# A planned attention and convolution kernel: other durations and weights in the planner, and one score unit for the last 64 keys of two chunks

## The chip, the cores and the metric

The kernel runs on one core of one Trainium2 chip. The metric is the device time of one execution in microseconds (us). An execution has five instruction streams: TensorE (PE in the profile, with its weight loads PEld), VectorE (DVE), ScalarE (ACT), GpSimd (POOL) and SyncE (SP).

## The reference

Two stages, in eight batches of 3136 rows:

```python
scores = (1/S) * z @ z.T                  # z: 3136 x 64
attn   = maximum(scores, 0) ** 2
x      = u * (attn @ v)                   # u, v: 3136 x 256
x1, x2, x3 = split(x @ w_proj, 3)         # 256 columns each
conv   = irfft(rfft(x2) * rfft(filter))   # along the 3136 rows
out    = (x1 * conv * x3) @ w_out
```

There is no softmax: a score is taken through ReLU and squared, and the score matrix is symmetric.

## The kernel before

**Tiles.** The 3136 rows are 25 tiles of 128 keys. The last tile (`NT - 1`, number 24) holds only 64 keys; its other 64 partitions carry the same keys again. The rows are also cut into seven chunks of queries, `CHUNKS = (512, 512, 512, 512, 512, 256, 320)`. A batch goes through its chunks in order.

**Score units.** For each chunk `entries(c)` (L1448) lists the key tiles in units, mostly two tiles to a unit. `score_mm` (L1484) multiplies 64 rows of z by the chunk's columns, one tile into each of the two PSUM banks of a pair. The 64 contraction rows fill half of the array: the first tile of a unit uses the upper half, the second the lower half. ScalarE applies ReLU to both banks in one instruction (L1672, PSUM into the tile `R`), and ScalarE or VectorE squares it (L1679 or L1681, `R` into `A`, bf16). Part of the score blocks come from the symmetry instead, by DMA transposes (`mirror`, L1583).

**Weighing.** `weigh` (L1500) multiplies `A` with v into two PSUM accumulators `ps_o`, one for each half of v's columns. The 64 keys of tile 24 are weighed apart by `weigh_short` (L1627), two half-array matmuls for a chunk, appended to the score group that comes `DELAY = 4` groups after the unit with tile 24 (`ends_at`, L1620). VectorE takes the accumulators out, in two halves, with the factor u (L1722, into `xT`).

**The last tile in chunks 0 to 3.** In these chunks tile 24 is a unit of its own, `(24,)`, in the middle of the chunk's list: one matmul, one bank used of the pair that it takes, a ReLU and a square over 512 columns.

**The second stage.** `add_proj` (L1023) projects `xT` (ReLU-free copies by either engine at L498 and L502, the gate product by VectorE in two halves at L1059), `add_spectrum` (L1113) and `add_end` (L1224) do the convolution by two-step transforms and the output projection. This is work of the kinds FA, FB and FZ, in the same streams as the scores (S) and the weighing (W).

**The planner.** The order of every stream is made when the program is built. Each piece of work is a `Task` with a cost on each engine that could run it, what it depends on, and the buffers that it takes. `Plan.go` (L309) runs the tasks through a model in time and emits them in the order that results. Its costs are linear: `c_act(n)`, `c_dve(n)`, `c_pe(n)` (L44 to L57). Going from S to other PE work or back adds a constant (L325). What the diff touches:

- `pick_pe` (L247) chooses PE's next task. While in S it stays there as long as the next score task can start within `STAY`; from other work it enters S when two pairs of banks are free, three where the W work on hand is over `AMPLE`; while it waits for pairs it takes W, and F work too where W on hand is over `BACKLOG`. F goes ahead of W while a credit is positive, which each W task raises by `PACE`, and while the queued work of ScalarE and VectorE (`queued`, L243) is under `FULL`.
- `pick` (L287) gives work that two engines could do to the second of them if it ends there earlier than on the first; `YIELD` adds the wait that this would cause to work that only that engine can do.
- `both` (L507) gives such work its two costs. The squares name VectorE first (L1688), nearly all PSUM copies ScalarE first.

Of the kernel before, what the change touches and what calls it, by code (L numbers as in the profile page):

```python
# [21 lines left out]
KR = 2 * N2  # L22
KC = 100
CHUNKS = (512, 512, 512, 512, 512, 256, 320)
PACE = 0.6
HOLD = 3
DELAY = 4
GROUP = 1
BACKLOG, AMPLE, STAY = 2.0, 4.0, 0.1
LATE_PUT, LATE_LOAD, LATE_TURN, LATE_C, LATE_D2 = 3.0, 1.0, 1.5, 2.5, 1.0  # L30
SPEC_LAG = 1
LATE_F = 6.0
# [1 line left out]
FINAL = (0, 2, 4, 6, 1, 3, 5)  # L34
ZP, ZL = 0, 0.0
MOST = 3
FULL = 3.0
YIELD = 1.0
REACH = 2
INF = float("inf")  # L40
ISSUED = "issued"


def c_act(n):  # L44
    return 0.055 + n * 0.000833


def c_dve(n):
    return 0.068 + n * 0.00104
# [110 lines left out]
class Plan:  # L160
# [148 lines left out]
    def go(self):  # L309
        while True:  # L310
            got = []
            x = self.pick_pe()
            if x:
                got.append((x[0], 0, x[1], "PE", x[2]))
            for i, e in enumerate(self.pend):
                x = self.pick(e)
                if x:
                    got.append((x[0], i + 1, x[1], e, None))
            if not got:
                break  # L320
            start, _, task, e, k = min(got, key=lambda g: g[:2])
            if k:
                self.queues[k].remove(task)
                if (k == "S") != (self.mode == "S") and self.mode:
                    start += 0.11  # L325
                self.mode = k
                if k == "W":
                    self.credit = min(self.credit + PACE, 2.0)
                elif k != "S":
                    self.credit = max(self.credit - task.cost["PE"], -2.0)  # L330
            self.run(task, e, start)
        left = sum(len(q) for q in self.queues.values()) + sum(len(q) for q in self.pend.values())
        assert not left, f"{left} tasks left over"
# [3 lines left out]
def kernel(  # L337
# [56 lines left out]
    v_p = Pool("v16", 2, [P, VW], BF16)  # L394
    R_p = Pool("R", 2, [P, 2, 512], F32)
    A_p = Pool("A", 8, [P, 1024], BF16)
    M_p = [Pool("M1", 1, [P, 2048], BF16), Pool("M2e", 1, [P, 2048], BF16), Pool("M2o", 1, [P, 2048], BF16)]
    xT_p = Pool("xT", 8, [P, 2, 512], BF16)
    g_p = Pool("gate", 26, [P, 512], BF16)
    x1_p = Pool("x1", 2, [P, 512], BF16)  # L400
    x2_p = Pool("x2", 2, [P, 2 * D], BF16)
    s1_p = Pool("s1", 3, [P, 2, D], BF16)
# [89 lines left out]
    def on(engine, emit, cost, deps=(), takes=(), **kw):  # L492
        return job(None, lambda e: emit(), {engine: cost}, deps, takes, **kw)
# [529 lines left out]
    def add_proj(b, c, xt, xt_tasks):  # L1023
# [7 lines left out]
        def to_gates():  # L1031
            for nb in range(2):
                box = {}

                def mm1(nb=nb, box=box):
                    box["p"] = bank()
                    box["x"] = x1_p.tile()
                    for k in range(2):
                        matmul(
                            box["p"][:, :cw], wp16[:, k, ds(nb * P, P)], xt["t"][:, k, :cw],  # L1040
                            start=(k == 0), stop=(k == 1),
                        )

                def ev1(e, box=box):
                    box["made"] = copy(e, box["x"][:, :cw], box["p"][:, :cw])

                def mm3(nb=nb, box=box):
                    box["p3"] = bank()
                    gates[b, c, nb] = g_p.tile()
                    for k in range(2):  # L1050
                        matmul(
                            box["p3"][:, :cw], wp16[:, k, ds((4 + nb) * P, P)], xt["t"][:, k, :cw],
                            start=(k == 0), stop=(k == 1),
                        )

                def ev3(nb=nb, box=box):
                    for h, w in halves(c):
                        g, p, x = (by_half(y, h, w) for y in (gates[b, c, nb], box["p3"], box["x"]))
                        got = nc.vector.tensor_tensor(g[:, ::-1] if h == 0 else g, p, x, ALU.mult)  # L1059
                        made.setdefault((b, c, nb), []).append(has_read(got, p, [box["made"]]))  # L1060

                a = pe(kind, mm1, c_pe(cw, cw), xt_tasks, [one_slots, x1_p.slots])
                if late and c in AFTER:
                    put_back.append(a)
                e1 = job(None, ev1, both(cw), [a], prio=late)
                e1.frees.append((a, 0))
                a3 = pe(kind, mm3, c_pe(cw, cw), [*xt_tasks, a], [one_slots, g_p.slots])
                e3 = on("DVE", ev3, c_dve(cw), [a3, e1], prio=late)
                e3.frees += [(a3, 0), (a, 1)]
                users.extend([a, a3])  # L1070
                gtasks.append((a3, e3))
# [375 lines left out]

    def entries(c):  # L1448
        skip = [t for a in mirrored(c) for t in tiles[a]]
        todo = [t for t in range(NT) if t not in skip]  # L1450
        pairs = []
        for a in range(c + 1, min(c + REACH, NC - 1) + 1):
            pairs += [tuple(tiles[a][i : i + 2]) for i in range(0, len(tiles[a]) - 1, 2)]
        rest = [t for t in todo if all(t not in x for x in pairs)]
        wide = 4 if 4 * CHUNKS[c] <= 1024 else 2
        rest = [tuple(rest[i : i + wide]) for i in range(0, len(rest), wide)]
        sends = [x for x in rest if any(c < home[t] <= c + REACH for t in x)]
        pairs = sorted(pairs + sends, key=lambda x: min(home[t] for t in x if home[t] > c))
        rest = [("S", x) for x in rest if x not in sends]
        pairs = [("S", x) for x in pairs]  # L1460
        taken = [("M", tuple(tiles[a][i : i + 2])) for a in mirrored(c) for i in range(0, len(tiles[a]), 2)]
        mid = [x for x in rest + pairs if NT - 1 in x[1]]
        rest, pairs = ([x for x in got if x not in mid] for got in (rest, pairs))
        h = len(rest) // 2
        if not pairs:
            got = spread(rest, taken)
            i = got.index(rest[h])
            return got[:i] + mid + got[i:]
        return spread(rest[:h], taken) + mid + spread(rest[h:], pairs)
# [6 lines left out]
    groups = [scored[i : i + GROUP] for i in range(0, len(scored), GROUP)]  # L1476
    mirrors, mirror_tasks = {}, {}

    def blocks(x, n, cw):
        if n <= 2:  # L1480
            return x[:, 0:n, :cw]
        return x[:].rearrange("p i j -> p (i j)")[:, 0 : n * cw].rearrange("p (i j) -> p i j", i=n)

    def score_mm(un, where):  # L1484
        b, c, k = un
        cw = CHUNKS[c]
        ps = ps_t[where]
        zt = zT[b]
        pair = plans[b, c][k][1]
        order = (0, 1) if len(pair) <= 2 else (0, 2, 1, 3)  # L1490
        for i in order[: len(pair)] if len(pair) != 3 else (0, 2, 1):
            t, h, m = pair[i], ds((i if len(pair) <= 2 else i // 2) * dqk, dqk), P
            matmul(
                blocks(ps, len(pair), cw)[:m, i], zt[h, ds(t * P, m)], zt[h, ds(C0[c], cw)], start=True, stop=True
            )
        live[un] = ps

    acc, full = {}, {}
# [121 lines left out]
    ends_at, scored_by = {}, {}  # L1620
    for gi, g in enumerate(groups):
        for b, c, k in g:
            if NT - 1 in plans[b, c][k][1]:
                ends_at.setdefault(min(gi + DELAY, len(groups) - 1), []).append((b, c))
    short, chunk_w, tails = {}, {}, {}

# [10 lines left out]
    for gi, g in enumerate(groups):  # L1637
# [15 lines left out]
            for x in more:  # L1653
                weigh_short(*x)

        costs = [c_pe(CHUNKS[un[1]]) for un in g]
        extra = sum(c_pe(CHUNKS[c]) for _, c in more)
        st = pe("S", sg, sum(costs) + extra, deps, [pair_slots] * len(g))
        tails[gi] = st
# [1 line left out]
        for i, un in enumerate(g):  # L1661
            b, c, k = un
            cw = CHUNKS[c]
            pair = plans[b, c][k][1]
            rows, n = P, len(pair)
            last = k == len(plans[b, c]) - 1
            box = {}

# [2 lines left out]
                p = blocks(live[un], n, cw)[:rows]  # L1671
                has_read(nc.scalar.activation(blocks(box["R"], n, cw)[:rows], p, AF.Relu), p)  # L1672

            def sq(e, un=un, rows=rows, n=n, cw=cw, box=box):
                A = A_p.tile()
                r = blocks(box["R"], n, cw)[:rows]
                a = A[:rows, 0 : n * cw].rearrange("p (i j) -> p i j", i=n)
                if e == "ACT":
# [6 lines left out]
                "ACT", relu, c_act(n * cw), [(st, -sum(costs[i + 1 :]) - extra)], [R_p.slots], prio=0  # L1685
            )
            r_.frees.append((st, i))
            how = {"DVE": c_dve(n * cw)} if (b, c) == (0, 0) and k > 1 else both(n * cw, "DVE")  # L1688
            q_ = job(None, sq, how, [r_], [A_p.slots], prio=1)
            q_.frees.append((r_, 0))  # L1690
            if c == NC - 1 and last or gi == len(groups) - 1:
                if b == 0:
# [1 line left out]
                else:  # L1694
                    st.frees.append((z_tasks[b][0], 0))
            mirror(un, q_)
            if NT - 1 in pair:
                short[b, c] = q_, un, pair.index(NT - 1)
            if all(x == "M" for x, _ in plans[b, c][:k]):
                for j in range(k):  # L1700
                    add_mirrored((b, c, j))
# [5 lines left out]
            if last:  # L1707
# [3 lines left out]
                for dh in range(2):  # L1711

                    def xe(dh=dh, b=b, c=c, cw=cw, xt=xt):
# [8 lines left out]
                            nc.vector.scalar_tensor_tensor(x, f, inv_s2, ut, ALU.mult, ALU.mult)  # L1722

                    x_ = on(
                        "DVE", xe, c_dve(cw), [w_last[dh], u_tasks[b, c], *((d, ISSUED) for d in evs)], [xT_p.slots] if dh == 0 else [], prio=-1
                    )
                    evs.append(x_)
                    x_.frees.append(w_first[dh])
# [45 lines left out]
    for gi, got in ends_at.items():  # L1774
        for b, c in got:
# [3 lines left out]
                join(tails[gi], t, ISSUED)  # L1779
            for t in chunk_w[b, c][1]:  # L1780
                join(t, tails[gi], ISSUED)
            if plans[b, c][un[2]][1] != (NT - 1,):
                q_.holders += 1
            tails[gi].frees.append((q_, 0))
    plan.go()
# [30 lines left out]
```

## Time and profile before

| what | value |
|---|---|
| three runs | 1015.51, 1019.09, 1020.16 us (median 1019.09) |
| the profiled execution | 1017.42 us |
| its span, first to last instruction | 1015.6 us |
| granted TensorE clock, mean | 0.998 |
| busy in the span | POOL 188.3 us (19%) |
| DMA | 170.18 MB, 168 GB/s mean |
| ReLU 128x1024, ACT, L1672 | 392 at 1027 ns |
| ReLU 128x512, ACT, L1672 | 48 at 603 ns |
| square 128x1024, DVE, L1681 | 254 at 1220 ns |
| square 128x1024, ACT, L1679 | 138 at 1068 ns |
| square 128x512, DVE / ACT | 25 at 687 ns / 23 at 639 ns |

How to read it: a duration in such a row is that of one record. Records of one engine overlap, because the next instruction starts before the one ahead of it is written back. What an instruction costs its engine in a stream is the time from its start to the start of the next. The difference between span and time (1.8 us) lies outside the first and last instruction.

### The profile page before, as it was taken

To read this page: it belongs to the slowest core of one execution; us is meant where nothing else is said; L and a number is where in the kernel's file an instruction comes from. 1 tells how busy PE (TensorE), PEld (TensorE's weight loads), DVE (VectorE), ACT (ScalarE), POOL (GpSimd) and SP (SyncE) were. 2 spreads that over 40 slices of the span, in tenths; PEclk is the share of its full clock that TensorE was granted. 3 is DMA by queue.
4 is the path that set the end of the run, shared out by engine and by line. 5 is a ranking of instruction groups with operands and counts; after the bars stand their busy time and mean duration, and the time that the engine had idled before them with its cause. 6 is when DMAs were issued, how large, how long until landed. Compare 5 with 4: busy or idle time off the path is not lost. (4 is left out here: it accounts for less than half of the span.)

```text
span 1015.6 us, 17745 instructions
## 1 busy us (share of the span) xinstructions
PE 980.1 (97%) x6046; PEld 493.1 (49%) x6046; DVE 821.6 (81%) x1440; ACT 882.6 (87%) x1247; POOL 188.3 (19%) x401
## 2 busy tenths in 40 slices
PE   6999999999999999999999999999999999999986
PEld 2344644446444554445544464444644455544664
DVE  7977779877789787897789878887788977898674
ACT  5877899987989889888999898999888989998884
POOL 5142311123111310222012131112201132000000
PEclk9999999999999999999999999999999999999999
DMA  9699878888678799888988789696888979978756
GB/s 169 127 181 171 157 137 147 170 177 184 139 155 171 139 181 207 163 151 149 208 187 167 140 182 210 129 186 133 179 193 155 191 130 170 213 165 172 126 183 210
DMA packets 331770, 170.18 MB, mean 168 GB/s; under 512 B 241160, under 2 KB 306504, under 8 KB 331680
## 3 DMA queue, kind: packets, MB, share of 16 engines
q1 hardware_dynamic: 303952, 138.09, 63.0%
q0 software_dynamic: 27728, 30.97, 20.8%
q8 instruction: 47, 0.77, 0.3%
q14 instruction: 43, 0.35, 0.1%
HBM read 90.26 MB, written 53.35 MB: 141 GB/s over the span
## 5 line engine op out<-in xcount | busy, mean ns | idle before, releaser
L1672 ACT ACTIVATE R_t<-ps_s 128x1024 f32<-128x1024 f32 (+3 forms) x528 | 473.0, 932 | 71.0 <-PE ps_s L465 52.9
L465 PE MATMUL ps_o_t<-A_t,v_t 128*128 128x512 bf16 (+4 forms) x2128 | 480.4, 355 | 4.1 <-DVE A_t L1681 3.3
L1681 DVE TENSOR_TENSOR A_t<-R_t 128x1024 bf16<-128x1024 f32 (+3 forms) x334 | 366.5, 1114 | 113.0 <-ACT R_t L1672 112.2
L465 PEld LDWEIGHTS <-v_t 128*128 128x128 bf16 (+1 forms) x2826 | 253.5, 98 | 265.0 <-issue 65.3
L1679 ACT ACTIVATE A_t<-R_t 128x1024 bf16<-128x1024 f32 (+4 forms) x194 | 184.4, 955 | 2.5
L465 PE MATMUL ps_s<-zT_t 64*128 64x512 bf16 (+2 forms) x1064 | 152.6, 356 | 4.1 <-ACT s_t L498 1.7
L548 POOL COPY tick<-xT_t 1x1 bf16<-1x1 bf16 x54 | 13.8, 256 | 729.3 <-DVE xT_t L1722 713.2
L465 PE MATMUL ps_s<-xT_t,wp 128*128 128x512 bf16 (+2 forms) x430 | 102.6, 352 | 2.7 <-DVE xT_t L1722 1.3
L498 ACT ACTIVATE x_t<-ps_s 128x512 bf16<-128x512 f32 (+2 forms) x148 | 79.6, 573 | 25.4 <-PE ps_s L465 17.7
L1722 DVE SCALAR_TENSOR_TENSOR xT_t<-ps_o_t,uT_t 128x256 bf16<-128x256 f32 (+2 forms) x224 | 76.3, 382 | 21.3 <-PE ps_o_t L465 16.4
L465 PEld LDWEIGHTS <-zT_t 64*128 64x128 bf16 (+1 forms) x1081 | 44.8, 95 | 97.0 <-issue 78.6
L1158 DVE TENSOR_TENSOR xh<-xh,H 100x1024 bf16<-100x1024 bf16 x120 | 80.9, 685 | 3.0 <-ACT xh L498 2.2
L465 PE MATMUL ps_o_t<-M_t,v_t 128*128 128x512 bf16 (+2 forms) x352 | 82.2, 353 | 0.0
L1059 DVE TENSOR_TENSOR gate_t<-ps_s,x_t 128x256 bf16<-128x256 f32 (+2 forms) x214 | 71.1, 383 | 12.9 <-PE ps_s L465 11.0
L465 PEld LDWEIGHTS <-wp 128*128 128x128 bf16 x448 | 42.5, 97 | 45.7 <-issue 8.9
L539 POOL DMA_DIRECT2D un_t<-in_u_dram x112 | 59.9, 557 | 9.8 <-issue 5.7
L1252 DVE TENSOR_TENSOR yT_t<-ps_s,gate_t 128x512 bf16<-128x512 f32 (+2 forms) x97 | 58.2, 623 | 3.1 <-PE ps_s L465 2.6
L558 POOL DMA_DIRECT2D v_t<-in_v_dram x112 | 59.5, 554 | 6.0 <-issue 1.7
L465 PE MATMUL ps_s<-wp,xT_t 128*128 128x256 bf16 x398 | 56.4, 272 | 0.4 <-DVE gate_t L1059 0.2
L465 PE MATMUL ps_s<-wo,yT_t 128*128 128x256 bf16 (+1 forms) x366 | 54.2, 273 | 1.3 <-DVE yT_t L1252 0.9
L498 ACT ACTIVATE s_t<-ps_s 128x512 bf16<-128x512 f32 (+1 forms) x79 | 45.2, 587 | 9.4 <-PE ps_s L465 4.3
L498 ACT ACTIVATE xh<-ps_s 100x512 bf16<-100x512 f32 (+1 forms) x90 | 51.8, 611 | 1.6 <-PE ps_s L465 1.4
(148 smaller groups left out, 842.3 us busy)
## 6 DMA issues: line engine op xcount, KB each, us to landing
out_dram<-ost_t SPq DMA_DIRECT2D x66, 256.0 KB
spec<-s_t SPq DMA_DIRECT2D x96, 128.0 KB
spec_in_t<-spec SPq DMA_DIRECT2D x28, 392.0 KB
spec<-gs_t SPq DMA_DIRECT2D x28, 392.0 KB
v_t<-in_v_dram POOLq DMA_DIRECT2D x80, 128.0 KB, 4.1
un_t<-in_u_dram POOLq DMA_DIRECT2D x80, 128.0 KB, 4.5
conv_in_t<-spec SPq DMA_DIRECT2D x33, 256.0 KB
out_dram<-ost_t SPq DMA_DIRECT2D x19, 128.0 KB
```

The costliest lines, as they stand in the source:

```text
L465: wrote(nc.tensor.matmul(o, *args, **kw), o)
L498: got = nc.scalar.activation(out_, in_, AF.Copy)
L539: nc.gpsimd.dma_start(out=t[ds(j * N1, N1), lo - t0 : hi - t0, :], in_=x[:, n2 : n2 + hi - lo, :])
L548: nc.gpsimd.tensor_copy(tick[:], xt["t"][0:1, 1, 0:1])
L558: nc.gpsimd.dma_start(out=t[ds(j * N1, N1), ds(v_at(a), (b - a) * D)], in_=r[:, n2 + a - lo : n2 + b - lo, :].rearrange("p t d -> p (t d)"),)
L1059: got = nc.vector.tensor_tensor(g[:, ::-1] if h == 0 else g, p, x, ALU.mult)
L1158: nc.vector.tensor_tensor(x[:, 1 - i], x[:, 0], h, ALU.mult)
L1252: got = nc.vector.tensor_tensor(yb["y"][:, dh, 0:w], p, gates[b, c, dh][:, 0:w], ALU.mult)
L1672: has_read(nc.scalar.activation(blocks(box["R"], n, cw)[:rows], p, AF.Relu), p)
L1679: nc.scalar.activation(a, r, AF.Square)
L1681: nc.vector.tensor_tensor(a, r, r, ALU.mult)
L1722: nc.vector.scalar_tensor_tensor(x, f, inv_s2, ut, ALU.mult, ALU.mult)
```

## The change

1. *Durations.* The constant for going in or out of S falls from 0.11 to 0.095. The VectorE tasks that are two half instructions (L1059, L1722) cost 0.064 us more. A score group costs 0.008 us more on PE for each unit, a square on ScalarE 0.039 us more.
2. *Weights.* `PACE` 0.6 to 0.5, `BACKLOG` 2.0 to 1.5, `AMPLE` 4.0 to 5.0, `STAY` 0.1 to 0.05, `FULL` 3.0 to infinity, `YIELD` 1.0 to 0.
3. *Sharing.* `SHARE = {0: 1, 2: 3}`: the unit `(24,)` of chunk 0 also scores tile 24 for chunk 1, and that of chunk 2 for chunk 3. The two blocks go to the two halves of the array and the two banks of the pair; ReLU and square take 1024 columns at once. Chunks 1 and 3 have no unit `(24,)`. The result goes into a buffer of its own, `As`, one of them, which is held until both chunks have weighed it. The second chunk's short weighing is appended `DELAY` groups after the middle of its own list.
4. *Buffers.* The pool of gates has 25 tiles, not 26.

```diff
-PACE = 0.6
+PACE = 0.5
-BACKLOG, AMPLE, STAY = 2.0, 4.0, 0.1
+BACKLOG, AMPLE, STAY = 1.5, 5.0, 0.05
-FULL = 3.0
-YIELD = 1.0
+FULL = INF
+YIELD = 0.0
+SHARE = {0: 1, 2: 3}
...
-                    start += 0.11
+                    start += 0.095
...
+    As_p = Pool("As", 1, [P, 1024], BF16)
-    g_p = Pool("gate", 26, [P, 512], BF16)
+    g_p = Pool("gate", 25, [P, 512], BF16)
...
-                e3 = on("DVE", ev3, c_dve(cw), [a3, e1], prio=late)
+                e3 = on("DVE", ev3, c_dve(cw) + 0.064, [a3, e1], prio=late)
...
-        todo = [t for t in range(NT) if t not in skip]
+        todo = [t for t in range(NT) if t not in skip and not (t == NT - 1 and c in SHARE.values())]
...
+    def parts(un):
+        b, c, k = un
+        pair = plans[b, c][k][1]
+        return [(t, c) for t in pair] + ([(NT - 1, SHARE[c])] if c in SHARE and pair == (NT - 1,) else [])
...
-            t, h, m = pair[i], ds((i if len(pair) <= 2 else i // 2) * dqk, dqk), P
-            matmul(
-                blocks(ps, len(pair), cw)[:m, i], zt[h, ds(t * P, m)], zt[h, ds(C0[c], cw)], start=True, stop=True
-            )
+            (t, at), h = pair[i], ds((i if len(pair) <= 2 else i // 2) * dqk, dqk)
+            matmul(blocks(ps, len(pair), cw)[:, i], zt[h, ds(t * P, P)], zt[h, ds(C0[at], cw)], start=True, stop=True)
...
-            if NT - 1 in plans[b, c][k][1]:
+            mine = [i for i, x in enumerate(plans[b, c]) if x[0] == "S"]
+            half_way = c in SHARE.values() and k == mine[len(mine) // 2]
+            if NT - 1 in plans[b, c][k][1] or half_way:
                 ends_at.setdefault(min(gi + DELAY, len(groups) - 1), []).append((b, c))
...
-        costs = [c_pe(CHUNKS[un[1]]) for un in g]
+        costs = [c_pe(CHUNKS[un[1]]) + 0.008 for un in g]
...
-            rows, n = P, len(pair)
+            rows, n = P, len(parts(un))
+            a_p = As_p if n > len(pair) else A_p
...
-            how = {"DVE": c_dve(n * cw)} if (b, c) == (0, 0) and k > 1 else both(n * cw, "DVE")
-            q_ = job(None, sq, how, [r_], [A_p.slots], prio=1)
+            how = {"DVE": c_dve(n * cw)} if (b, c) == (0, 0) and k > 1 else {"DVE": c_dve(n * cw), "ACT": c_act(n * cw) + 0.039}
+            q_ = job(None, sq, how, [r_], [a_p.slots], prio=1)
...
-                        "DVE", xe, c_dve(cw), [w_last[dh], u_tasks[b, c], *((d, ISSUED) for d in evs)], [xT_p.slots] if dh == 0 else [], prio=-1
+                        "DVE", xe, c_dve(cw) + 0.064, [w_last[dh], u_tasks[b, c], *((d, ISSUED) for d in evs)], [xT_p.slots] if dh == 0 else [], prio=-1
```

More of the change, by code (lines that the diff above doesn't have):

```diff
@@ L24 @@
 CHUNKS = (512, 512, 512, 512, 512, 256, 320)
-PACE = 0.6
+INF = float("inf")
+PACE = 0.5
 HOLD = 3
@@ L36 @@
 MOST = 3
-FULL = 3.0
-YIELD = 1.0
+FULL = INF
+YIELD = 0.0
 REACH = 2
-INF = float("inf")
+SHARE = {0: 1, 2: 3}
 ISSUED = "issued"
@@ L1488, in score_mm @@
         zt = zT[b]
-        pair = plans[b, c][k][1]
+        pair = parts(un)
         order = (0, 1) if len(pair) <= 2 else (0, 2, 1, 3)
         for i in order[: len(pair)] if len(pair) != 3 else (0, 2, 1):
-            t, h, m = pair[i], ds((i if len(pair) <= 2 else i // 2) * dqk, dqk), P
-            matmul(
-                blocks(ps, len(pair), cw)[:m, i], zt[h, ds(t * P, m)], zt[h, ds(C0[c], cw)], start=True, stop=True
-            )
+            (t, at), h = pair[i], ds((i if len(pair) <= 2 else i // 2) * dqk, dqk)
+            matmul(blocks(ps, len(pair), cw)[:, i], zt[h, ds(t * P, P)], zt[h, ds(C0[at], cw)], start=True, stop=True)
         live[un] = ps
@@ L1672, in relu, with sq @@
                 has_read(nc.scalar.activation(blocks(box["R"], n, cw)[:rows], p, AF.Relu), p)
-            def sq(e, un=un, rows=rows, n=n, cw=cw, box=box):
-                A = A_p.tile()
+            def sq(e, un=un, rows=rows, n=n, cw=cw, box=box, a_p=a_p):
+                A = a_p.tile()
                 r = blocks(box["R"], n, cw)[:rows]
@@ L1696 @@
             mirror(un, q_)
-            if NT - 1 in pair:
-                short[b, c] = q_, un, pair.index(NT - 1)
+            for i_, (t, at) in enumerate(parts(un)):
+                if t == NT - 1:
+                    short[b, at] = q_, un, i_
             if all(x == "M" for x, _ in plans[b, c][:k]):
@@ L1781 @@
                 join(t, tails[gi], ISSUED)
-            if plans[b, c][un[2]][1] != (NT - 1,):
+            if plans[b, un[1]][un[2]][1] != (NT - 1,) or un[1] != c:
                 q_.holders += 1
```

## The prediction, made before the changed kernel was run

> **What bounds the kernel now.** I read the head of the page first, then the groups with their shapes kept apart, then PE in order of time, then PE's waits.
>
> ```profile
> span 1015.6 us, 17745 instructions
> PE 980.1 (97%) x6046; PEld 493.1 (49%) x6046; DVE 821.6 (81%) x1440; ACT 882.6 (87%) x1247; POOL 188.3 (19%) x401
> ```
>
> TensorE carries the time, but its 97% are records that overlap, so neither the 980 us of work nor the 35 us of idle time can be taken as they stand. The order of time shows what a matmul costs the stream:
>
> ```profile
> 136.76 0.38 PE L465 MATMUL ps_s<-spec_in_t,S 98*100 98x512 bf16 x1
> 136.98 1.03 PE L465 MATMUL ps_o_t<-A_t,v_t 128*128 128x512 bf16 x4
> 137.94 0.82 PE L465 MATMUL ps_s<-zT_t 64*128 64x512 bf16 x6
> 138.69 1.04 PE L465 MATMUL ps_o_t<-A_t,v_t 128*128 128x512 bf16 x4
> ...
> 141.82 0.61 PE L465 MATMUL ps_s<-zT_t 64*128 64x512 bf16 x4
> 142.44 0.59 PE L465 MATMUL ps_o_t<-A_t,v_t 128*128 128x512 bf16 x2
> 143.57 1.46 PE L465 MATMUL ps_o_t<-A_t,v_t 128*128 128x512 bf16 x6 [0.54 <-DVE A_t L1681]
> 144.96 0.82 PE L465 MATMUL ps_s<-zT_t 64*128 64x512 bf16 x5
> 145.71 0.60 PE L465 MATMUL ps_o_t<-A_t,v_t 128*128 128x512 bf16 x2
> ```
>
> Three prices are in it. One full-array matmul over 512 columns stands 0.22 us before the next (136.76 to 136.98), though its record lasts 0.38; start to start in the trace it is 216 ns, and 136, 109 and 55 ns for 320, 256 and 128 columns. Six score matmuls take 0.82 us, and five take 0.82 as well: the two of a unit run side by side on the halves of the array (their starts lie 4 ns apart in the trace), so one alone costs what two do. And going in or out of half-array work costs extra: the four matmuls from 136.98 account for 0.86 us, to 137.84, and the scores start at 137.94; three pairs account for 0.65, to 138.59, and the weighing starts at 138.69. The trace has 92 to 96 ns for nearly every such passage; I use 94.
>
> With these prices the list of instructions of the kernel before holds 795.2 us of full-array and 117.5 us of half-array matmuls and 404 passages (38.0 us): 950.6 us. PE's first matmul starts at 4.75 us, its last ends at 1007.5. So about 52 us between them are waits and small steps, against some 22 that the idle time on PE between these ends shows: a wait under about 0.16 us hides in the record ahead of it. The waits by stage, start to start: 9.6 us up to 30 us, 6.4 after 980, and about 31 in between. The answer on PE's waits for the middle (30 to 900 us) names less, the tops being
>
> ```profile
> PE ps_s L465 <- ACT s_t L498: 2.0, 2, 1.7
> PE ps_o_t L465 <- DVE A_t L1681: 1.7, 4, 0.6
> PE ps_o_t L465 <- DVE xT_t L1722: 1.7, 4, 0.8
> PE ps_s L465 <- DVE xT_t L1722: 1.3, 4, 0.6
> ```
>
> Its rows sum to 9.5 us, 5.5 of them for results of VectorE and 4.0 of ScalarE, spread over many short ones. There is no one wait to remove; at most 31 us lie in the middle for any order to win.
>
> Here the Trainium skill speaks (Perfetto Trace Analysis, Identifying the Most-Contended Engine): matmul busy time is no measure of the distance to the roofline, because pipelined matmuls look different in a trace; its substitute is the share of the weight loads. The trace agrees with the first half (35 us of idle time against about 65 outside the counted 950.6); by the second half, 49%, half of the span would be to win, which the start-to-start sum does not bear out.
>
> **Sharing, what it removes.** In each of eight batches two units `(24,)` go: 16 score groups with one block. The list of the changed kernel has 576 pairs and 25 lone half-array matmuls where before has 560 and 57. Sixteen slots of 216 ns are 3.5 us of PE work, on the stream that sets the time. The weighing keeps its matmuls (6046 in both). Sixteen fewer units also take a pair of PSUM banks.
>
> ReLU: 32 instructions over 512 columns become 16 over 1024. Records: 2 x 603 - 1027 = 179 ns each; start to start 2 x 477 - 904 = 50 ns, so 0.8 us of ScalarE, and 1 to 3 us more for the squares of both engines together. That lies beside PE; I count nothing for it. The buffer `As` is one, but it is read for the last time about half a chunk into the second chunk, and next written in the middle of the chunk after that: half a chunk is about 9 us (1016 / 56 / 2), against 2.3 us for the ReLU and square that fill it, so I count no wait. If that cover failed, the square and all that is behind it on its engine would wait, up to 9 us in each of the 15 places where the buffer is taken again. One gate tile fewer: 14 are made in a batch, and 25 hold eleven of the next while the old ones are used, so it costs nothing, or at the worst one wait in a batch of 0.8 us (the second longest in that answer), 6 us in all. No DMA is added or removed: SP and POOL have the same 635 and 406 instructions.
>
> **Weights, what they add.** The changed list has 213 half-array runs, not 202 (shorter stays in S outweigh the 16 groups gone), so 426 passages: 22 x 94 ns = 2.1 us more. PE's counted work is 950.6 - 3.5 + 2.1 = 949.2.
>
> This is the second place for the Trainium skill (TensorEngine Tiling, Key Properties): a change of the tiling mode drains the array, which speaks against an order that changes it more often. It gives no time; the 94 ns agree with it. Without that rule the sum would be 2.1 us lower.
>
> **What moves between ACT and DVE.** By the lists, ScalarE does 203 squares over 1024 columns instead of 138, and 34 over 640 instead of 22; some 58 copies of 512 columns go the other way. At start-to-start prices (ReLU 904 ns, square 947 on ScalarE and 1133 on VectorE, copy 477 and 601) ScalarE goes from 829 to 861 us, VectorE from 794 to 756. Nothing of it is on the path as such: PE has 949. In stretches of 10 us of PE work, laid every 5 us from 30 to 910, ScalarE is given more than 10 us in 32 of 174, against 21; the excess sums to 6.9 us against 5.2, for VectorE 1.6 against 1.4. So this costs between nothing and, if all 32 us of it came on the path, 32; nearest is the difference of the excesses, 2 us.
>
> **What true durations are worth.** The old plan had squares on ScalarE 39 ns short (908 for 947), 194 times: 7.6 us. It had the two-half instructions 62 ns short (600 for 2 x 331), 224 tasks at most: 14 us, on the engine for which 5.5 of the 9.5 us were waited. The passages were 16 ns too dear, the units 8 ns too cheap, which about cancels (-6 and +4 us). An order written for results that come 22 us too early over the run makes PE wait where slack is thin. So the gain lies between nothing (slack hid it all, or other results come late) and 22 us. The slack says that it is thin in few places: PE work between a score and its weighing, less ReLU, square and 0.2 us for each hand-over (an estimate), is under 0.5 us for 24 of about 1980 matmuls before and 19 after, median 5.5 and 6.6 us; for matmuls that read `xT` 33 and 28 of about 1115; for those on `yT` worse, 9 and 18 of 324. I take 7 off, a little under a quarter of the 31 and a third of the 22, and give 2 back for ScalarE: 5.
>
> **Sum.** Profiled execution 1017.4 - 3.5 + 2.1 - 5 = 1011.0 us. The median of the three runs is 1.7 us above that execution, which I do not carry over. A measurement of this kernel can tell about 0.5% from no change: faster means under 1014.0, slower over 1024.2, both against the median 1019.1.
>
> **Rivals.**
>
> - *The forecast*, 1006 to 1015, chance 0.45. For it: fewer PE slots by count, truer durations, slack no worse at the weighing. Against it: the gain in waits is chosen between wide bounds.
> - *Only the counted work moves.* New waits replace old ones (the `yT` slack points there), or a side effect such as the gate tile eats the gain: 1017.4 - 1.4 = 1016, 1014 to 1020. Chance 0.27. A case in point is that the sharing doesn't act, because the two blocks aren't side by side: 1017.4 + 2.1 = 1019.5; the lists speak against it, since the two matmuls have the two halves of the array.
> - *The waits of the middle fall by half*: 1017.4 - 1.4 - 16 = 1000, 996 to 1006. Chance 0.09. For it: 22 us of mispriced work. Against it: slack that hardly changes.
> - *Slower: ScalarE becomes the bound.* Only it does the ReLU, and a pair of banks is free only after it. With `FULL` infinite, F work no longer stops while copies queue up, and with `YIELD` 0 squares go to ScalarE in front of waiting ReLUs. Its place is the attention stretches where ScalarE is given over 10 us in 10; it decides from where these follow each other, so that the excess isn't worked off. If a third to a half of the 32 us came on PE: +11 to +16, so 1027 to 1032 with the counted work. Chance 0.19, a few hundredths of it under 1024.2. Against it: VectorE has 38 us less, and in stretches of 25 us ScalarE passes PE in only 3 of 69.
>
> So faster 0.52, within 0.5% 0.31, slower 0.17. The range 1000 to 1025 leaves out about 0.04 below and 0.16 above.
>
> **What would show it.** Right: five-matmul score groups nearly gone, ReLU 128x1024 at 408 and 128x512 at about 16 records, 0.10 us at each passage; PE's waits for `A`, `xT` and gates shorter; the start-to-start waits in the middle at some 26 us. ACT's busy time should rise by about 30 us and DVE's fall by about 38. Wrong: ReLU waiting behind squares, with PE's scores waiting for `R` (now 0.5 us in the middle), says ScalarE; a wait of the `As` square for PE says the one buffer; PE waiting for `gate` or `yT` says the gate tile and the thinner slack.

## The result, and the profile after

The changed kernel takes 1011.84 us (median of 6 runs, 1010.03 to 1013.70), the kernel before, run along, 1018.67: ratio 0.9943, 95% interval 0.9929 to 0.9957, or 5.8 us less. The forecast was 1011.0. The profiled execution has 1012.86 us and is the second slowest of the six; before's had 1017.42.

The head of the page after:

```profile
span 1011.0 us, 17656 instructions
PE 967.4 (96%) x5958; PEld 490.8 (49%) x6046; DVE 787.6 (78%) x1424; ACT 907.9 (90%) x1231; POOL 188.7 (19%) x401
```

PE's busy time seems to have fallen by 13 us. That can't be read so: 88 of 6046 matmul records are missing, while all weight loads are there. So I compare stretches that need no single record: the time from the first matmul's start to the last one's end, less the work counted from the list of instructions. Before that is 1002.8 - 950.6 = 52.2 us of waits and small steps, after 998.4 - 949.2 = 49.2. Of the 4.4 us between these stretches, 1.4 are counted work and 3.0 waits. Each of these figures is of one execution, and the six executions of the changed kernel lie up to 3.7 us apart.

In PE's order of time the groups with one lone block are nearly gone (groups of five matmuls over 512 columns: 34 before, 7 after), and a group with a shared unit takes what any three pairs take:

```profile
48.31 0.59 PE L468 MATMUL ps_o_t<-M2e_t,v_t 128*128 128x512 bf16 x2
48.84 0.82 PE L468 MATMUL ps_s<-zT_t 64*128 64x512 bf16 x6
49.59 1.04 PE L468 MATMUL ps_o_t<-M2e_t,v_t 128*128 128x512 bf16 x4
```

The groups by shape show the ReLU at 408 instructions over 1024 columns (392 before), and the squares, of which VectorE did 254 and ScalarE 138, shared evenly (another eight on each engine go into `As`):

```profile
L1681 ACT ACTIVATE R_t<-ps_s 128x1024 f32<-128x1024 f32 x408 | 406.5, 1031 | 27.2 <-PE ps_s L468 24.3 <-DVE A_t L1690 1.0 <-DVE As_t L1690 0.2
L1690 DVE TENSOR_TENSOR A_t<-R_t 128x1024 bf16<-128x1024 f32 x197 | 238.6, 1221 | 110.9 <-ACT R_t L1681 110.0
L1688 ACT ACTIVATE A_t<-R_t 128x1024 bf16<-128x1024 f32 x195 | 207.8, 1070 | 2.6
```

Behind the second bar stands the idle time before the instructions and what ended it. The row of the large ReLU before:

```profile
L1672 ACT ACTIVATE R_t<-ps_s 128x1024 f32<-128x1024 f32 x392 | 390.7, 1027 | 60.4 <-PE ps_s L465 46.4 <-DVE A_t L1681 9.5 <-issue 1.3
```

ScalarE waits less for scores in front of the large ReLU (24.3 us, 46.4 before); it has more of its own to do. PE's waits from 30 to 900 us:

```profile
PE ps_s L468 <- ACT ost_t L501: 2.7, 2, 2.2
PE ps_s L468 <- DVE xT_t L1732: 2.4, 6, 0.7
PE ps_o_t L468 <- DVE A_t L1690: 2.3, 4, 0.9
PE ps_o_t L468 <- issue: 1.9, 12, 0.2
PE ps_s L468 <- ACT R_t L1681: 1.4, 4, 0.5
```

The row "issue" is what missing records leave; before, with all its records, has none. Without it the whole list sums to 9.7 us, where before had 9.5. The tops are others: a wait of 2.2 us for an output copy, where one of 1.7 for a spectrum copy stood; the ReLU (`R`) has gone from 0.5 to 1.4 us. So the waits that the profile names moved, and the 3.0 us came off the short ones that hide in the records. Laying the list of instructions on the trace gives them by stage, small steps included: up to 30 us they fall from 9.7 to 8.9 us, in the middle from 35.6 to 33.0, and in the 27.5 us before the end of the last matmul they rise from 6.4 to 6.9.

### The profile page after: what moved, and what is told of

The parts are those of the page before. It is cut to its first block, busy times and chain, and to the rows that moved or that the text cites. A ratio compares the mean times of both kernels' runs of the same rounds, so it can differ in the third digit from the quotient of the medians.

```text
span 1011.0 us, 17656 instructions
## 1 busy us (share of the span) xinstructions
PE 967.4 (96%) x5958; PEld 490.8 (49%) x6046; DVE 787.6 (78%) x1424; ACT 907.9 (90%) x1231; POOL 188.7 (19%) x401
## 4 chain that ended last, share of the span: by engine, by line
PE 76%; DVE 8%; ACT 8%; issue 3%; DMA 3%; SPq 1%; ACTq 0%; DVEq 0%
PE ps_o_t L468 42%; PE ps_s L468 33%; ACT R_t L1681 5%; DVE A_t L1690 3%; ACT A_t L1688 2%; DVE xh L1161 1%; DVE xT_t L1732 1%; DMA out_dram<-ost_t 1%; DMA ost_t<-in_z_dram 1%; DMA M_t<-A_t 1%; DMA A_t<-spec 1%; SPq L593 1%; DVE yT_t L1255 0%; DVE R_t L1161 0%; ACT s_t L501 0%
## 5 line engine op out<-in xcount | busy, mean ns | idle before, releaser
L1681 ACT ACTIVATE R_t<-ps_s 128x1024 f32<-128x1024 f32 (+4 forms) x512 | 471.0, 958 | 43.9 <-PE ps_s L468 40.3
L468 PE MATMUL ps_o_t<-A_t,v_t 128*128 128x512 bf16 (+3 forms) x1998 | 461.7, 353 | 8.9 <-DVE A_t L1690 4.0
L468 PEld LDWEIGHTS <-v_t 128*128 128x128 bf16 x2826 | 254.3, 98 | 254.3 <-issue 59.4
L1690 DVE TENSOR_TENSOR A_t<-R_t 128x1024 bf16<-128x1024 f32 (+3 forms) x250 | 280.0, 1130 | 123.3 <-ACT R_t L1681 122.0
L1688 ACT ACTIVATE A_t<-R_t 128x1024 bf16<-128x1024 f32 (+3 forms) x246 | 243.2, 995 | 4.6 <-DMA M_t<-A_t 1.3
L468 PE MATMUL ps_s<-zT_t 64*128 64x512 bf16 (+2 forms) x1064 | 148.7, 356 | 4.8 <-ACT ost_t L501 2.7
L501 ACT ACTIVATE x_t<-ps_s 128x512 bf16<-128x512 f32 (+2 forms) x143 | 77.2, 572 | 15.4 <-PE ps_s L468 9.3
L505 DVE CAST x_t<-ps_s 128x512 bf16<-128x512 f32 (+2 forms) x70 | 44.6, 648 | 9.0 <-PE ps_s L468 7.1
```

Source lines behind the costliest of these rows:

```text
L468: wrote(nc.tensor.matmul(o, *args, **kw), o)
L501: got = nc.scalar.activation(out_, in_, AF.Copy)
L505: got = nc.vector.tensor_copy(out_, in_)
L1688: nc.scalar.activation(a, r, AF.Square)
L1690: nc.vector.tensor_tensor(a, r, r, ALU.mult)
```

## The experiments

My theory, A: the time follows PE's counted work plus waits, and true durations in the plan shorten the waits. The rivals: B, the gain is in the weights; C, any edit draws a new order, whose waits scatter by several us; and later D, the ReLUs on ScalarE set the pace and PE's slots hardly count. Twelve kernels were run. All but four have an order of their own, since an edit of a cost or weight makes the planner write another. "Counted" is PE's work from the list of instructions at the prices of the prediction; "rest" is first to last matmul in the profiled execution less the counted work. Each ratio is against before in the same job. The rest is of one execution and shares its scatter: the kernel with the shared unit on one half has 5.2 us less of it than the changed kernel in the same order, and was not faster.

| kernel | ratio, 95% interval | counted | rest |
|---|---|---|---|
| before | 1 | 950.6 | 52.2 |
| changed | 0.9943 (0.9929 to 0.9957) | 949.2 | 49.2 |
| sharing alone | 0.9989 (0.9973 to 1.0004) | 946.6 | 53.1 |
| durations alone | 0.9969 (0.9954 to 0.9984) | 952.7 | 46.3 |
| weights alone | 0.9973 (0.9958 to 0.9988) | 952.3 | 46.7 |
| changed without sharing | 1.0055 (1.0036 to 1.0075) | 953.5 | 57.9 |
| the same, `PACE` 0.49 | 1.0011 (1.0001 to 1.0022) | 953.8 | 51.6 |
| changed, `PACE` 0.49 | 0.9945 (0.9933 to 0.9958) | 948.3 | 49.9 |
| before, `PACE` 0.61 | 1.0035 (1.0021 to 1.0048) | 952.5 | 56.3 |
| sharing and durations, weights of before | 0.9921 (0.9909 to 0.9933) | 947.9 | 46.3 |
| changed, shared unit on one half of the array | 0.9956 (0.9943 to 0.9968) | 952.7 | 44.0 |
| changed, 12 us more ScalarE | 0.9963 (0.9949 to 0.9977) | 949.2 | 51.0 |
| changed, 16 us more VectorE | 0.9955 (0.9942 to 0.9968) | 949.2 | 48.0 |
| changed, 13.8 us more TensorE | 1.0040 (1.0026 to 1.0055) | 963.1 | 43.0 |

### The three parts, one at a time, and all but one

**Sharing alone**: the changed kernel with

```diff
-PACE = 0.5
+PACE = 0.6
-BACKLOG, AMPLE, STAY = 1.5, 5.0, 0.05
+BACKLOG, AMPLE, STAY = 2.0, 4.0, 0.1
-FULL = INF
-YIELD = 0.0
+FULL = 3.0
+YIELD = 1.0
```

and the five durations of before.

> Only the sharing (with the As buffer and 25 gate tiles); durations and weights as before. Theory A (PE's counted matmul work plus waits that true durations shorten): the list of this kernel counts 946.6 us of PE work against 950.6 before (576 pairs, 25 lone half-array matmuls, 398 passages), waits unchanged, so 4 us less than before: ratio 0.996. Rival B (the gain is in the weights, the rest is nothing): 1.000. Rival C (the order of the plan is luck, any edit moves the waits by several us): anything from 0.992 to 1.008.

Measured: 1015.93 us, 1.1 us under before, the interval taking in no change. The counted 4 us came to a quarter.

**Durations alone**: the weights of before, `SHARE = {}`, 26 gate tiles.

> Only the durations; no sharing, weights and 26 gate tiles as before. Theory A: counted PE work 952.7 us (+2.1, 426 passages instead of 404), waits shorter by about 7, so 5 us less than before: ratio 0.995, and the waits in the middle, start to start, at about 27 us instead of 34. Rival B: 1.000 to 1.002, waits as before. Rival C: 0.994 to 1.010.

Measured: 1014.82 us, 3.2 us less, although PE has 2.1 us more counted work. The rest fell from 52.2 to 46.3 us, in the middle from 35.6 to 30.7. The time fell by two thirds of what theory A expected. That is what its mechanism would give, but one order can't show it: the next run has nearly the same rest, 46.7 us, without the true durations.

**Weights alone**: the durations of before, `SHARE = {}`, 26 gate tiles.

> Only the weights; old durations, no sharing, 26 gate tiles. Theory A: counted PE work 952.3 us (+1.7), ScalarE 862 us instead of 829 with an excess over 10-us stretches of 8.1 us instead of 5.2, so 4 to 5 us more than before: ratio 1.004. Rival B (the weights are what gains): 0.993 to 0.996, since VectorE has 36 us less to do and the two together 3.6 us less. Rival C: 0.996 to 1.010.

Measured: 1014.49 us, 2.8 us less. Theory A is wrong here in sign; rival B came nearer, and C's range holds the value. ScalarE did take the squares,

```profile
L1681 ACT ACTIVATE R_t<-ps_s 128x1024 f32<-128x1024 f32 x392 | 391.0, 1030 | 37.8 <-PE ps_s L468 33.4 <-DVE A_t L1690 1.6 <-issue 1.0
L1690 DVE TENSOR_TENSOR A_t<-R_t 128x1024 bf16<-128x1024 f32 x201 | 243.7, 1222 | 114.0 <-ACT R_t L1681 113.3
L1688 ACT ACTIVATE A_t<-R_t 128x1024 bf16<-128x1024 f32 x191 | 203.7, 1070 | 2.4
```

but the idle time before the large ReLU that VectorE's squares end is 1.6 us, where before has 9.5.

**Changed without sharing**:

```diff
-SHARE = {0: 1, 2: 3}
+SHARE = {}
```

> The changed kernel without the sharing (no As buffer, 26 gate tiles); durations and weights as changed. Theory A: counted PE work 953.5 us against 949.2 in the changed kernel and 950.6 before; waits 3 us less than before as in the changed kernel: about as before, ratio 0.999 to 1.000, and 4 to 6 us over the changed kernel. Rival B: the gain stays, 0.994 to 0.996. Rival C: 0.990 to 1.005, with no relation to the counted work.

Measured: 1022.23 us, 10.4 us over the changed kernel (11.4 by the ratios) and 5 over before; its twelve executions spread from 1019.61 to 1027.49. None of the theories but C has room for it: durations and weights each win 3 us alone, and together they lose 5.

### Empty changes

**The changed kernel with `PACE` 0.49, before with 0.61, and the run without sharing with 0.49**, each an edit of one hundredth:

> The changed kernel with PACE 0.49 instead of 0.50: a change with no meaning of its own that gives another order. Counted PE work 948.3 us against 949.2, ScalarE 856 us against 861. Theory A: 0 to 1 us less, 1011, ratio 0.9935. Theory C (the waits are drawn anew with every order, with a scatter of several us): off the changed kernel by 2 to 8 us, most likely above it, 1013 to 1019.

> The kernel before with PACE 0.61 instead of 0.60, as empty a change. Counted PE work 952.5 us against 950.6 (424 passages against 404), ScalarE and VectorE within 1.3 us. Theory A: 2 us more, ratio 1.002. Theory C: within 8 us on either side, ratio 0.992 to 1.008.

> The run without the sharing (durations and weights as changed, 1022.2 us) with PACE 0.49 instead of 0.50. Counted PE work 953.8 us against 953.5. If the sharing is worth 10 us in this plan for a reason of its own, 1022 again (ratio 1.005). If that run had a bad order (theory C), nearer to what the counted work says, 1014 to 1018 (ratio 0.997 to 1.001).

Measured: 1011.83, 1021.05 and 1018.65 us. The first does nothing (0.2 us). The second costs 3.6 us for 1.9 us of counted work, and the third wins 4.5 us against its twin for 0.3 us more. So an order can be 2 to 5 us better or worse for no reason that the edit names. Of the 10 to 11 us of the run without sharing over the changed kernel, 4 to 5 come and go with such an edit. Differences of 3 us between kernels with different orders, one by one, prove nothing about the edit.

### The same order with one thing more

These four keep the order of the changed kernel, so scatter of orders is out. The first:

```diff
-            (t, at), h = pair[i], ds((i if len(pair) <= 2 else i // 2) * dqk, dqk)
+            (t, at), h = pair[i], ds((0 if n_same(un) else i if len(pair) <= 2 else i // 2) * dqk, dqk)
```

with `n_same` true for a shared unit.

> The changed kernel, but the two score matmuls of the shared unit both use the upper half of the array (the key tile is there twice), so they can't run side by side; the order of every engine is that of the changed kernel. Theory A (the sharing saves 216 ns of TensorE time 16 times because the two run side by side): 3.5 us over the changed kernel's 1011.8, so 1015 (ratio to before 0.998), in the profile three matmuls' time where two blocks of a shared unit and a pair took two. Rival (what the sharing gains are banks and ScalarE's instructions, the array's halves don't matter, or waits swallow it): 1012, ratio 0.9945.

The order of time of this run, at the group shown above:

```profile
48.24 0.59 PE L468 MATMUL ps_o_t<-M2e_t,v_t 128*128 128x512 bf16 x2
48.77 1.04 PE L468 MATMUL ps_s<-zT_t 64*128 64x512 bf16 x6
49.73 1.04 PE L468 MATMUL ps_o_t<-M2e_t,v_t 128*128 128x512 bf16 x4
```

The six matmuls take 0.22 us more, and the weighing starts 0.96 us after them instead of 0.75. So the saving is real at its place. But the time is 1012.41 us: by the ratios 1.3 us over the changed kernel, not 3.5, with an interval of about 2 us either way. To see whether slots of PE are worth less than their time, larger doses went on each engine:

```diff
                 has_read(nc.scalar.activation(blocks(box["R"], n, cw)[:rows], p, AF.Relu), p)
+                dose_n[0] += 1
+                if dose_n[0] % 4 == 0:
+                    nc.scalar.activation(dose_t[0][:], dose_t[0][:], AF.Copy)
```

```diff
                     nc.vector.tensor_tensor(a, r, r, ALU.mult)
+                    nc.vector.tensor_copy(dose_t[1][:], dose_t[1][:])
```

```diff
-            (t, at), h = pair[i], ds((i if len(pair) <= 2 else i // 2) * dqk, dqk)
+            (t, at), h = pair[i], ds((0 if c == 4 else i if len(pair) <= 2 else i // 2) * dqk, dqk)
```

> The changed kernel, in its own order, with one copy of 128x1 added on ScalarE behind every fourth ReLU: 128 x 94 ns = 12 us of ScalarE (861 to 873 us by start-to-start prices), nothing on TensorE or VectorE. Theory A (TensorE's slots set the time, the other engines work beside it): 0 to 3 us over 1011.8. Theory D (TensorE's slots are not what the time follows, since 3.5 us more of them cost 0.6 us; the ReLUs on ScalarE set the pace): 8 to 12 us more, 1020 to 1024.

> The changed kernel, in its own order, with one copy of 128x1 added on VectorE behind every square there: 250 x 65 ns = 16 us of VectorE (756 to 772 us), nothing elsewhere. Theory A and theory D: 0 to 3 us over 1011.8. If VectorE's results are what PE waits for (its rows lead PE's waits), 8 to 16 us more.

> The changed kernel, in its own order, with both score matmuls of every unit of chunk 4 and of the shared units' kind there on the upper half of the array, so that they run one after the other: 64 slots of 216 ns, 13.8 us of TensorE (949.2 to 963.1 us), nothing on ScalarE or VectorE. Theory A: 13 to 14 us over 1011.8, 1025.5. Theory D: 2 to 6 us, 1014 to 1018, the waits of PE taking up the rest, as in the run with 3.5 us.

Measured: 1013.74, 1012.40 and 1021.43 us. Against the changed kernel's ratio that is 2.0 us for 12 of ScalarE, 1.2 for 16 of VectorE and 9.9 for 13.8 of TensorE. Per us of work: TensorE 0.7 (0.55 to 0.9 by the intervals), ScalarE 0.17 (0 to 0.33), VectorE 0.07 (below 0.2). Theory D falls: TensorE sets the time. But theory A is too simple as well, for part of the added work goes where PE would have waited: the rest falls from 49.2 to 43.0 us in the run with the TensorE dose. The heads of its page and of the ScalarE dose's show what landed: weight loads and PE's busy time up in the first, 128 instructions and 9 us on ACT in the second (of the 12; its records overlap):

```profile
span 1019.1 us, 17656 instructions
PE 980.0 (96%) x5958; PEld 496.7 (49%) x6046; DVE 789.1 (77%) x1424; ACT 910.3 (89%) x1231; POOL 188.8 (19%) x401
```

```profile
span 1012.8 us, 17786 instructions
PE 970.4 (96%) x5958; PEld 491.2 (49%) x6046; DVE 787.6 (78%) x1426; ACT 916.7 (91%) x1359; POOL 188.8 (19%) x401
```

### A version that these prices point to

With them the weights look like a loss: 32 us more on ScalarE at 0.17 are 5 us, 38 us less on VectorE at 0.07 win 3. The intervals of both prices reach down to nothing, and that work taken away wins what added work costs is assumed. So the weights alone were undone:

> The changed kernel with the weights of before (sharing, As buffer, 25 gate tiles and durations as changed). Counted PE work 947.9 us (412 passages) against 949.2 in the changed kernel, ScalarE 826 us against 861, VectorE 795 against 756. Theory A with the slot at the 0.7 that the dose of TensorE work showed: 1 us under the changed kernel for PE, 5 under it for ScalarE's 35 us at 0.16, 3 over it for VectorE's 39 us at 0.07: 1008 to 1010, ratio 0.991 to 0.9925, the best of all. If the new weights are needed to turn the sharing into time: 1013 to 1016, ratio 0.996 to 0.999. If the scatter of orders covers it: between 0.990 and 0.998 with no relation to the counts.

Measured: 1009.24 us (6 runs, 1008.59 to 1010.06), the fastest of all, 8.0 us under before and 2.2 under the changed kernel by the ratios, whose intervals just overlap. Its page and its waits of PE from 30 to 900 us:

```profile
span 1006.8 us, 17708 instructions
PE 975.4 (97%) x6046; PEld 491.2 (49%) x6046; DVE 821.7 (82%) x1436; ACT 879.0 (87%) x1219; POOL 188.5 (19%) x401
```

```profile
PE ps_o_t L468 <- DVE xT_t L1732: 2.2, 4, 1.3
PE ps_s L468 <- ACT R_t L1681: 1.4, 5, 0.4
PE ps_o_t L468 <- DVE A_t L1690: 1.1, 3, 0.6
PE ps_o_t L468 <- ACT A_t L1688: 1.0, 4, 0.3
```

The rest is 46.3 us, 3 less than in the changed kernel; no wait of 2 us for a copy is in it. Whether that is the weights or a good order, one run of one order cannot say; the forecast from the doses (1008 to 1010) held.

## Why the prediction was right, point by point

- **What bounds it.** TensorE, with waits around it: shown by the doses. The unspoken half of the sum, that a us of PE work is a us of time, was not right; it is about 0.7.
- **Sharing, 3.5 us.** The slots went (576 pairs, 25 lone, groups of six at 0.82 us), and the run on one half of the array shows the 0.22 us for each at its place. In time they are worth 2 to 3 us at the price of the large dose, 1.3 at their own measurement. In different orders the sharing moved the time by 1.1 us (old plan), 4.9 (true durations: 0.9969 to 0.9921) and 7 to 11 (durations and weights). What lies over 3 us there is not explained by slots; 16 units fewer also hold 16 pairs of banks less and 0.8 us of ReLU. How much is that and how much order stays open.
- **Passages, 2.1 us.** 426 in the list, 94 ns each as before, so the count stood. The Trainium skill's rule (TensorEngine Tiling, Key Properties) that a change of mode drains the array agrees with the trace: in the rows of after above the weighing starts 0.75 us after the scores, whose three pairs account for 0.65. But the 94 ns are the trace's, so the sum would not be 2.1 us lower without that rule, as the prediction says.
- **True durations, 7 us.** Neither the size nor the sign is shown. With true durations the time fell by 3.2 us in the plan of before and by 6.9 with sharing and the weights of before (0.9989 to 0.9921). But with the new weights and no sharing it rose by 8.3 (0.9973 to 1.0055), or by 3.9 with `PACE` 0.49. Two signs that the prediction named did not come in the changed kernel: PE's named waits for `A` rose from 1.7 to 2.3 us and those for `xT` stayed at 3.0, only the 0.5 us for gates are gone; and the waits in the middle fell by 2.6 us, where it wanted 5. Sharing and new weights with the old durations, the run that would price the durations in the changed kernel, was not made.
- **ScalarE, 2 us back.** ACT's busy time rose by 25 us (30 forecast) and DVE's fell by 34 (38), so the squares moved as counted. In the final kernel the price was about right: 5 us for ScalarE less 3 for VectorE by the doses, 2.2 us measured when the weights were undone. In other plans it was not: with the false durations and no sharing the weights won 2.8 us, with the true ones and no sharing they cost 8.7 (0.9969 to 1.0055), or 4.3 with `PACE` 0.49. The expectation that they cost 4 to 5 us alone was wrong in sign; that for the run without the sharing (0.999 to 1.000, measured 1.0055) missed too. A guess for the first is that the old `YIELD` rule, fed with wrong costs, held back work that ScalarE could have done; it was not tried.
- **`As`, one buffer.** Nobody in PE's list waited for it. The view of this tile has 0.2 us in all:

```profile
L1690 DVE TENSOR_TENSOR As_t<-R_t x8: 1212/1220/1226, 21.8 to 889.6; 128x1024 bf16<-128x1024 f32 x8
L1688 ACT ACTIVATE As_t<-R_t x8: 1056/1076/1208, 168.0 to 848.9; 128x1024 bf16<-128x1024 f32 x8
...
who waited for it (us, times):
  ACT R_t L1681: 0.2, 1
```

- **The gate tile.** No wait of PE for a gate from 30 to 900 us; nothing, as taken.
- **The sum.** In the profiled executions the waits gave 3.0 us, the counted work 1.4; the forecast had 5 and 1.4. The medians lie 6.8 us apart, and the two profiled executions 4.6, one above its median and one below. The parts that the runs bear out are the bound, the slots and the passages, worth 1.4 us of counted work together. The other 5 us were put on durations and weights, whose effects change sign from plan to plan, and an edit of one hundredth moved the time by up to 4.5 us. So that the parts add up to 1011 is in good part luck. That scatter of orders belongs into a range, beside the mechanisms.

## What to carry to other kernels

Where a planner writes the order, an edit of its costs or weights is also a new draw of the order: run one or two empty edits first and see how far they move the time, and judge an edit of 3 us by several orders or by one that keeps the order. Doses of extra work on each engine in a fixed order give what a us is worth there, and here these prices pointed to the version that turned out fastest, though one run of one order can't show that they are why. Whether correct durations in a plan are worth their trouble was not settled here: they won in two plans and lost in a third.

## What the runs showed of the hardware that was not expected

Two half-array matmuls on the same half cost two slots, but the trace does not always show it where it happens. In the run on one half, where a group ends with the shared unit, the second matmul starts 216 ns after the first; where it begins with the unit, as in the rows above, the two starts are recorded about 10 ns apart, and the 0.2 us appear later in the group. In the run with the TensorE dose, opening pairs on one half show 10 ns in some groups and 226 in others. Measure such a group from its first start to the start of what follows it.
